# Infini-attention and GEGLU on one core: an order laid out with margins towards TensorE, score passes that share four PSUM banks, two buffers for phi of Q, and first projections that begin with high parts

## The chip, the cores and the metric

The kernel runs on one core of a Trainium2 chip. Its engines run side by side, each through its own list of instructions in program order: TensorE (PE, with a weight loader, PEld), VectorE (DVE), ScalarE (ACT), GpSimd (POOL) and SyncE (SP), which here issues the DMA transfers. They meet at semaphores. TensorE writes into PSUM, eight banks of 128 partitions by 512 float32 values; VectorE and ScalarE read them there. The metric is the device time of one execution in microseconds (us), as a median over runs.

## The reference

A layer norm, attention in four segments of 512 rows with a memory carried from segment to segment, a residual, a second layer norm, a feed-forward layer with a gate, a residual. There are 2048 rows of 512 features and 32 heads of 16 features; the feed-forward layer is 1376 wide.

```python
for s in range(N):                                   # N = 4 segments, L = 512
    qs, ks, vs = q[:, :, s], k[:, :, s], v[:, :, s]
    logits = jnp.einsum("bhqd,bhkd->bhqk", qs, ks) * scale + mask
    p = _softmax(logits, axis=-1)
    a_dot = jnp.einsum("bhqk,bhkd->bhqd", p, vs)
    pq = phi(qs)                                     # t + 1 above zero, else exp(t)
    num = jnp.einsum("bhld,bhde->bhle", pq, M)
    den = jnp.einsum("bhld,bhd->bhl", pq, z)[..., None] + 1e-6
    a_mem = num / den
    o = g * a_mem + (1.0 - g) * a_dot
    outs.append(o)
    pk = phi(ks)
    M = M + jnp.einsum("bhld,bhle->bhde", pk, vs)
    z = z + jnp.einsum("bhld->bhd", pk)
...
h = x + o @ wo
h2 = h + ((gelu(ln(h) @ w_gate) * (ln(h) @ w_up)) @ w_down)
```

All is float32. The kernel writes an operand as a high and a low part and makes a product of three matmuls (high·high, low·high, high·low; `SPLIT`).

## The kernel before

**Tiling.** Attention goes through 16 units: four groups of eight heads (`c`) by four segments (`s`), in the order of `UNITS`. A unit has two halves `Q` of four heads, 32 in all. For each unit `qkv` projects Q and K (`project`, L619: 12 matmuls of 512 columns each, for Q and for K), splits them into `hl` (L680 on ScalarE, L682 on VectorE), and spreads them by DMA over `stq` and `stk`, where a head's 16 features stand with the three parts of the split; `phi` (L627 to L631) makes the memory's feature map of Q (`pq`) and K (`pk`); `vproj` (L648) makes V for two units at a time, in `vaug`; L718 and L726 transpose phi of K and add to the memory; `mem` (L756, L772) reads it out.

**The score passes.** Each half `Q` has two. `pass_a` (L797) computes the scores once, and VectorE reduces each row to its maximum over the allowed keys (L807, 512 of them, which writes the masked scores to a scratch tile `junk` besides); the maxima are transposed (L830), copied and put into a spare row of `stq` by DMA, so that the second pass subtracts them inside its matmul. `pass_b` (L862, L869) computes the scores again, transposed; ScalarE takes the exponential out of the bank (L876), POOL zeroes what lies above the diagonal (L879), and TensorE multiplies by V in four column tiles at a time (`accum`, L900). ScalarE copies the result (L921), and it goes through DRAM to be divided by the sum.

**Banks.** A bank belongs to a pool: `PD` has three (projections, transposes, V and memory), `PA` two (scores of `pass_a`), `PB` two (scores of `pass_b`), `PPV` one (P·V). When a pool has no more use for its banks it hands them on to the feed-forward layer's pools (`PX`, `PYZ`).

**The end.** `wo_seg` (L973) multiplies by `wo`, adds the residual (L977) and stores it; `ln2` normalises, transposes (L579) and combines; `ffn` computes gate and up projections with seven block products instead of eight (L1145: 22 tiles, 42 matmuls each), with additions on VectorE (L1157) and copies on ScalarE (L1152), and the gate (L1163 to L1173); `down` (L1206, 528 matmuls) adds up in `pt` tiles (L1211).

**The start.** `ln1` normalises the rows of the first segment; its first call runs 17 transposes of no use (L497) on TensorE, then transposes the normalised rows into four banks (L568), three of `PD` and one of `PA`, and splits them into `xt` (ScalarE L588 the high part, VectorE L589 the low part).

**The order.** The program is not written in the order in which it runs. Each operation is handed to `Sched.op` with an engine, an estimated duration, a priority and its operands; `Sched.run` then plays it through and emits the instructions in the order in which they start in that play. A buffer (`Val`) takes a tile out of its pool (`Pool_`) when its first operation starts. Among the operations that could start within a short window the one of the lowest priority value goes. `DUE` shifts the priority of groups of operations (Q and K projections, DMAs, V, memory, the two passes, P·V and so on), one number for each unit or half. `LAT` is the planned time from the end of an operation on one engine to the start of its successor on another, `TAKEN` the time until its buffers are free. On the chip nothing of these times is executed: an instruction waits for its semaphores alone, in the order that came out.

## Time and profile before

| | us |
|---|---|
| median of 3 runs | 832.03 |
| lowest and highest | 831.11, 833.02 |
| profiled execution | 830.79 |
| its span, first to last instruction | 829.1 |

| engine | busy us in the span |
|---|---|
| TensorE, matmuls | 805.0 |
| TensorE, weight loads | 623.6 |
| VectorE | 612.0 |
| ScalarE | 563.5 |
| GpSimd | 484.2 |

A row of a group of instructions reads: line, engine, operation, output and inputs, shape, count, then busy time, mean ns of one, and the idle time of the engine ahead of them with what ended it. A row of the list of waits reads: who waited, for whom, us in total, number of waits, longest. A row of the timeline reads: start, length, engine, line, operation, count, and in brackets the idle time before it. A row of the windows reads: stretch, its length, then for PE, PEld, DVE, ACT and POOL the busy time and the number of instructions, the granted clock, the share of the DMA engines and GB/s. A matmul's end is modelled and reaches over the start of the next, so that busy time on PE also holds short waits; the distance from start to start is what it takes.

### The profile page before, as it was taken

Reading aid. Unit: us, or ns where it says so; the run is one execution under the profiler, and the core shown is the slowest. Engines: PE = TensorE matmul, PEld = TensorE weight load, DVE = VectorE, ACT = ScalarE, POOL = GpSimd, SP = SyncE. Lnnn points to the kernel's source line nnn. Section 1 sums busy time; section 2 is a strip of 40 time slices with the busy share of each in tenths; the row PEclk is TensorE's granted clock in tenths of the full one; section 3 lists DMA queues with packets and bytes.
Section 4 is the critical chain, followed back from the end, with each engine's and each line's share of the span. In section 5 each row is a group of like instructions: output and inputs, shape, how many; then the busy total and the mean of one; then the engine's idle time right before and its main releaser. Section 6 shows DMA issues by size and latency. Waiting matters only on the chain.

```text
span 829.1 us, 15346 instructions
## 1 busy us (share of the span) xinstructions
PE 805.0 (97%) x4709; PEld 623.6 (75%) x4709; DVE 612.0 (74%) x1831; ACT 563.5 (68%) x1127; POOL 484.2 (58%) x719
## 2 busy tenths in 40 slices
PE   5999999999999999999999999999999999999998
PEld 4877767777777677776667677777888887788886
DVE  7888678788895878888896874676568856756565
ACT  6877868689988768776776862787467464545551
POOL 7533433444445444544736895788697686778750
PEclk9999999999999999999999999999999999999999
DMA  6543534565456564556554665531111341212102
GB/s 229 148 133 94 153 108 130 151 182 155 118 156 177 159 154 119 154 152 169 165 163 144 200 200 166 164 115 48 55 55 48 95 162 51 65 39 63 51 1 102
DMA packets 71750, 103.52 MB, mean 125 GB/s; under 512 B 14324, under 2 KB 24884, under 8 KB 71668
## 3 DMA queue, kind: packets, MB, share of 16 engines
q1 hardware_dynamic: 71668, 102.54, 42.6%
q8 instruction: 37, 0.61, 0.3%
q14 instruction: 45, 0.37, 0.2%
HBM read 54.92 MB, written 21.43 MB: 92 GB/s over the span
## 4 chain that ended last, share of the span: by engine, by line
PE 77%; DVE 10%; ACT 4%; issue 3%; POOL 3%; DMA 2%; SPq 1%; ACTq 0%; POOLq 0%; DVEq 0%
PE bank L1145 19%; PE bank L1206 14%; PE bank L619 8%; PE bank L797 8%; PE bank L869 7%; PE bank L900 7%; PE bank L973 4%; PE bank L648 4%; DVE junk L807 3%; ACT pt L876 1%; PE bank L726 1%; POOL raw L1122 1%; PE bank L772 1%; PE bank L579 1%; DVE hl L682 1%
## 5 line engine op out<-in xcount | busy, mean ns | idle before, releaser
L807 DVE CUSTOM_DVE_ANT_0 junk<-bank,amask 128x256 f32<-128x256 f32 (+3 forms) x512 | 228.3, 485 | 43.4 <-PE bank L797 40.3
L879 POOL TENSOR_SCALAR_AFFINE_SELECT pt<-pt 128x128 f32<-128x128 f32 (+2 forms) x352 | 118.8, 346 | 191.6 <-ACT pt L876 183.5
L876 ACT ACTIVATE pt<-bank 128x512 f32<-128x512 f32 (+1 forms) x352 | 181.4, 560 | 42.8 <-PE bank L869 36.4
L797 PE MATMUL bank<-stk,stq 128*128 128x512 f32 (+2 forms) x384 | 128.1, 377 | 4.3 <-DVE nm L807 3.9
L869 PE MATMUL bank<-stq,stk 128*128 128x384 f32 (+2 forms) x384 | 110.8, 351 | 1.7 <-ACT pt L876 1.4
L619 PE MATMUL bank<-xt,w 128*128 128x512 f32 x384 | 108.4, 394 | 1.1 <-DVE xt L589 1.1
L1211 DVE TENSOR_TENSOR pt<-pt,bank 128x512 f32<-128x512 f32 x96 | 65.0, 685 | 41.7 <-PE bank L1206 40.1
L797 PEld LDWEIGHTS bank<-stk,stq 128*128 128x128 f32 x384 | 68.6, 188 | 28.4 <-DVE nm L807 13.8
L869 PEld LDWEIGHTS bank<-stq,stk 128*128 128x128 f32 x384 | 67.3, 188 | 19.9 <-ACT pt L876 8.3
L619 PEld LDWEIGHTS bank<-xt,w 128*128 128x128 f32 x384 | 70.4, 188 | 12.5 <-DVE xt L589 1.3
L900 PE MATMUL bank<-pt,vaug 128*32 128x512 f32 (+3 forms) x1024 | 77.0, 436 | 0.0
L900 PEld LDWEIGHTS bank<-pt,vaug 128*32 128x32 f32 x1024 | 28.9, 109 | 39.1 <-issue 30.2
L648 PE MATMUL bank<-wv,xt 128*128 128x256 f32 x384 | 54.9, 283 | 0.0
L648 PEld LDWEIGHTS bank<-wv,xt 128*128 128x128 f32 x384 | 52.2, 189 | 1.8 <-issue 0.2
L1145 PE MATMUL bank<-xt,w 128*128 128x512 f32 (+1 forms) x186 | 51.2, 391 | 0.4 <-DVE n L1171 0.4
L1115 POOL TENSOR_TENSOR w<-raw,w 128x512 fp32r<-128x512 f32 (+3 forms) x37 | 42.0, 1137 | 6.8 <-ACT w L1113 6.6
L435 POOL TENSOR_TENSOR w<-raw,w 128x512 fp32r<-128x512 f32 (+1 forms) x23 | 29.7, 1291 | 22.3 <-ACT w L430 22.1
L807 DVE DVE_READ_ACCUMULATOR2_ANT nm<- 128x1 f32 x512 | 42.0, 82 | 0.0
L1145 PEld LDWEIGHTS bank<-xt,w 128*128 128x128 f32 (+1 forms) x186 | 34.3, 186 | 8.9 <-ACT ge L1163 0.8
L1145 PE MATMUL bank<-stk,w 128*128 128x512 f32 (+1 forms) x138 | 38.8, 390 | 0.0
L1122 POOL TENSOR_TENSOR raw<-raw,raw 128x256 f32<-128x256 f32 (+1 forms) x44 | 35.2, 799 | 2.9
L1122 POOL TENSOR_TENSOR raw<-raw 128x256 f32<-128x256 f32 (+1 forms) x44 | 33.6, 765 | 1.8
(298 smaller groups left out, 1798.5 us busy)
## 6 DMA issues: line engine op xcount, KB each, us to landing
stq<-hl SPq DMA_DIRECT2D x96, 128.0 KB
stk<-hl SPq DMA_DIRECT2D x192, 64.0 KB
pv_dram<-pvs SPq DMA_DIRECT2D x32, 256.0 KB
r<-r_dram SPq DMA_DIRECT2D x28, 256.0 KB
row<-x SPq DMA_DIRECT2D x24, 256.0 KB
raw<-wg SPq DMA_DIRECT2D x20, 256.0 KB
raw<-wu SPq DMA_DIRECT2D x20, 256.0 KB
raw<-wd SPq DMA_DIRECT2D x20, 256.0 KB
```

Source lines behind the costliest of these rows:

```text
L619: nc.tensor.matmul(pm.t, w.t[:, wi, dc * P:(dc + 1) * P], XT[s][dc].t[:, xi, :], start=dc == 0 and n == 0, stop=dc == ND - 1 and n == 2)
L648: nc.tensor.matmul(pm.t[:, 256 * t:256 * t + 256], XT[s][dc].t[:, xi, t0:t0 + P], whl[wi].t[:, h, 256 * (dc % 2):256 * (dc % 2) + 256], st ...
L797: nc.tensor.matmul(sa.t[:, k * w:(k + n) * w].rearrange("x (n w) -> x n w", n=n), sq.t[:, p, i * P:(i + 1) * P], sk.t[:, p, a:a + n, 0:w], ...
L807: nc.vector.tensor_tensor_reduce(out=junk.t[:, :w], in0=sa.t[:, k * w:(k + 1) * w], in1=amask[:, D - w:], op0=OP.add, op1=OP.min, scale=-1 ...
L869: nc.tensor.matmul(sc.t[:, lo:lo + D - q0], sk.t[:, p, a, q0:q0 + P], sq.t[:, p, q0:D], start=True, stop=True)
L876: act(w, prio, lambda: nc.scalar.activation(e.t[:, :w], sc.t[:, :w], AF.Exp), [sc], [e])
L879: nc.gpsimd.affine_select(v, v, pattern=pat + [[1, P]], compare_op=OP.is_ge, fill=0.0, base=0, channel_multiplier=-1)
L900: nc.tensor.matmul(pv.t[32 * n:32 * n + 32, kb * P:D], va.t[:, kb, 17 * j:17 * j + 32], e.t[:, lo:lo + D - kb * P], start=kb == 0, stop=la ...
L1122: pool(0.14 + 2.13e-3 * h, prio, lambda: nc.gpsimd.tensor_tensor(d.t[:, d0:d0 + h], a.t[:, a0:a0 + h], c.t[:, c0:c0 + h], op=o), ins, [d])
L1145: nc.tensor.matmul(dst.t[:w], v.t[:, wi, c0 + j * w:c0 + (j + 1) * w], b[bk][j].t[:, xi, :], start=first and j == 0 and n == 0, stop=j == ...
L1206: nc.tensor.matmul(pm.t, HH[p, f, s][hi].t[:w, t * P:(t + 1) * P], v.t[:w, wi, :], start=f == fl[0] and n == 0, stop=f == fl[-1] and n == 2)
L1211: dve(D, prio, lambda a=a, pm=pm: nc.vector.tensor_tensor(a.t, a.t, pm.t, op=OP.add), [pm], [a])
```

## The change

- `DUE` has new numbers throughout.
- In `LAT`, the times from ScalarE, VectorE and GpSimd to TensorE are 0.4 us longer; in `TAKEN`, ScalarE and VectorE hold a buffer 0.1 us longer. Planned durations of the DMAs of 64 to 128 KB, of P·V and of the warm-up are others.
- `PA` and `PB` are one pool of four banks.
- `pass_a` writes the masked scores back into the score bank; `junk` keeps one buffer, for the layer norms. `pq` gets a second buffer; a scratch value of the start moves to the buffer of `e`; `pt` tiles are given out in order.
- The first layer norm runs 12 transposes of no use instead of 17, and its rows are transposed into three score banks and one of `PD`.
- Unit 0 projects Q and K together (`project_two`): for each block of features four matmuls with the high part of `xt`, then two with the low part.
- `phi` is given its output, which is taken when the projection starts.

```diff
 LAT = {
     "PE": {"PE": 0.0, "ACT": 0.27, "DVE": 0.246, "POOL": 0.24, "SP": 0.25},
-    "ACT": {"PE": 0.14, "ACT": 0.12, "DVE": 0.137, "POOL": 0.172, "SP": 0.12},
-    "DVE": {"PE": 0.108, "ACT": 0.12, "DVE": 0.17, "POOL": 0.165, "SP": 0.12},
-    "POOL": {"PE": 0.085, "ACT": 0.08, "DVE": 0.09, "POOL": 0.12, "SP": 0.12},
+    "ACT": {"PE": 0.54, "ACT": 0.12, "DVE": 0.137, "POOL": 0.172, "SP": 0.12},
+    "DVE": {"PE": 0.508, "ACT": 0.12, "DVE": 0.17, "POOL": 0.165, "SP": 0.12},
+    "POOL": {"PE": 0.485, "ACT": 0.08, "DVE": 0.09, "POOL": 0.12, "SP": 0.12},
 }
-TAKEN = {"PE": 0.22, "ACT": 0.14, "DVE": 0.12, "POOL": 0.1}
+TAKEN = {"PE": 0.22, "ACT": 0.24, "DVE": 0.22, "POOL": 0.1}
...
-    PA = Pool_(banks[3:5], then=PX)
-    PB = Pool_(banks[5:7], then=PYZ)
+    PA = PB = Pool_(banks[3:7], then=Parts(1, PX, PYZ, PX, PYZ))
...
-    PPT = Pool_(many("pt", 2, [P, D]), then=PACC)
+    PPT = Pool_(many("pt", 2, [P, D]), fifo=True, then=PACC)
     PROW1 = Pool_(many("pt1", 9, [P, D]), then=PPT)
-    PJ = Pool_(many("junk", 2, [P, D]), then=PC)
+    PJ = Pool_(many("junk", 1, [P, D]), then=PC)
     PE_ = Pool_(many("e", 1, [P, D]), then=PC)
-    PPQ = Pool_(many("pq", 1, [P, D]), then=PC)
+    PPQ = Pool_(many("pq", 2, [P, D]), then=PC)
...
-            pe(17 * 0.227, prio, lambda: [nc.tensor.transpose(
-                wm.t[0:24, 0:P], bn.t.rearrange("p t k -> p (t k)"), ident) for n in range(17)],
+            pe(12 * 0.21, prio, lambda: [nc.tensor.transpose(
+                wm.t[0:24, 0:P], bn.t.rearrange("p t k -> p (t k)"), ident) for n in range(12)],
...
-            pts = [Val(PA if dc == 3 else PD) for dc in range(ND)]
+            pts = [Val(pool_) for pool_ in ((PA, PA, PB, PD) if not behind else (PD, PD, PD, PA))]
...
+    def project_two(prio, w, s, acq):
+        pm = [Val(PD), Val(PD)]
+        for dc in range(ND):
+            def f(dc=dc):
+                for n, (i, wi, xi) in enumerate((i, wi, xi) for wis, xi in (((0, 1), 0), ((0,), 1))
+                                                for i in range(2) for wi in wis):
+                    nc.tensor.matmul(pm[i].t, w[i].t[:, wi, dc * P:(dc + 1) * P], XT[s][dc].t[:, xi, :],
+                                     start=dc == 0 and n in (0, 2), stop=dc == ND - 1 and n > 3)
+            pe(6 * mm(D), prio, f, [*w, XT[s][dc]], pm, acq=acq if dc == 0 else [])
+        return pm
...
-                junk = Val(PJ)
-
-                def g(k=k, a=a, p=p, junk=junk):
+                def g(k=k, a=a, p=p):
                     nc.vector.tensor_tensor_reduce(
-                        out=junk.t[:, :w], in0=sa.t[:, k * w:(k + 1) * w], in1=amask[:, D - w:],
+                        out=sa.t[:, k * w:(k + 1) * w], in0=sa.t[:, k * w:(k + 1) * w], in1=amask[:, D - w:],
                         op0=OP.add, op1=OP.min, scale=-1.0, scalar=BIG,
                         accum_out=nm.t[:, a, p, i:i + 1])
-                dve(w, prio, g, [sa, vamask], [junk, nm], chain=True)
+                dve(w, prio, g, [sa, vamask], [nm], chain=True)
```

## Prediction

> **What bounds the kernel now.** I read the page first, then the chain of waits in order of time, then the list of waits by engine, and last the timeline at the places that the change touches.

> ```profile
> span 829.1 us, 15346 instructions
> ...
> PE 805.0 (97%) x4709; PEld 623.6 (75%) x4709; DVE 612.0 (74%) x1831; ACT 563.5 (68%) x1127; POOL 484.2 (58%) x719
> ...
> PE   5999999999999999999999999999999999999998
> ...
> PEclk9999999999999999999999999999999999999999
> ```

> TensorE is the bound in every slice but the first, and its clock is granted in full. So the question is how much of its 805 us is work and how much is waiting that looks like work, since a matmul's recorded span contains the pipeline's tail. The unbroken stretches of the chain give the pace of each kind of matmul (columns: start, length, what):

> ```profile
> 7.61 3.58 PE bank L497 x17
> ...
> 106.33 2.29 PE bank L900 x32
> ...
> 141.69 0.71 PE bank L648 x6
> ...
> 225.60 0.87 PE bank L579 x8
> ...
> 236.19 0.86 PE bank L772 x2
> 237.99 0.93 PE bank L726 x8
> ...
> 601.84 12.26 PE bank L1145 x54
> ...
> 812.99 12.25 PE bank L1206 x54
> ```

> 12.26/54 is 0.227 us for a moving operand of 512 columns, 0.71/6 is 0.118 for 256, in proportion 0.170 for 384, and 0.87/8 is 0.109 for a transpose. The counts follow from the loops of the code. Of 512 columns: 384 (L619), 192 (L797), 128 (L869), 192 (L973), 924 (L1145) and 528 (L1206), together 2348, or 533.0 us. Of 384: 256, 43.5 us. Of 256: 640, 75.5 us. The P·V products L900: 32 groups of 2.29, 73.3 us. L726 and L772: 12 of 0.93 and 12 of 0.86, 21.5 us. Transposes 208, with the 48 short products of L756 counted as such (an upper bound), 27.9 us. The warm-up L497 3.4 us. The sum is 778 us. TensorE runs from 7.61 to 812.99 + 12.25 = 825.24, which is 817.6 us. So about 39.5 us are lost between matmuls, and that is all that an order can win: no matmul of the computation is removed. Where the named part of it lies:

> ```profile
> PEld bank L797 <- DVE nm L807: 13.8, 32, 1.7
> PEld bank L869 <- ACT pt L876: 8.3, 24, 1.0
> ...
> PEld bank L830 <- DVE pk L631: 2.4, 3, 1.6
> PEld bank L862 <- ACT pt L876: 2.3, 5, 0.9
> PEld bank L830 <- DVE mm L826: 1.6, 4, 0.5
> ...
> PEld bank L1145 <- ACT vaug L1152: 1.2, 2, 0.7
> ...
> PEld bank L1206 <- DVE ln L554: 1.0, 1, 1.0
> ```

> These are total, times and longest. The weight loader (PEld) waits for VectorE and ScalarE 71 times in these rows, 30.6 us, 0.43 us a time, nearly all in the two score passes. Its idle time is an upper bound of what TensorE loses, as a load may wait while an earlier matmul still streams. The lower bound is TensorE's own idle time: 829.1 − 805.0 = 24.1, less 7.6 before its first matmul and 3.9 after its last, leaves 12.6 us, 1.1 of it at the start (below), so 11.5.

> **The change part by part.**

> *Start (shorter warm-up, other banks for the transposed rows, the first two projections together).*

> ```profile
> 9.80 1.45 DVE L533 TENSOR_SCALAR pt<-pt,mv,ln 128x512 f32<-128x512 f32 x3
> 9.92 0.82 ACT L545 ACTIVATE pt<-pt,ln,ln 128x512 f32<-128x512 f32 x1 [0.52 <-DVE ln L539]
> ...
> 11.02 1.91 PE L568 MATMUL bank<-ident,pt 128*128 128x128 f32 x16
> ...
> 12.64 2.07 ACT L588 ACTIVATE xt<-bank 128x512 fp32r<-128x512 f32 x4 [1.91 <-PE bank L568]
> ...
> 13.27 2.48 DVE L589 TENSOR_TENSOR xt<-bank,xt 128x512 fp32r<-128x512 f32 x4 [1.42 <-ACT xt L588]
> 14.02 5.75 PE L619 MATMUL bank<-xt,w 128*128 128x512 f32 x24 [1.08 <-DVE xt L589]
> ```

> The transposes L568 start when the 17 warm-up transposes are through, at 11.02. Five fewer, at 3.58/17 = 0.21, end them about 1.05 us earlier; but the third normalised row is ready only at 9.80 + 1.45 = 11.25, and eight transposes (0.87) stand behind it, so the last ends near 12.15 rather than 12.64: 0.45 us. Then L619 waits 1.08 us for the first low part (13.27 + a quarter of 2.48, and the way), because its bank is one that the transposed rows hold. In the changed order those rows lie in three score banks and one projection bank, both projections find free banks, and four matmuls of high parts come ahead of the first with a low one (4 × 0.227 = 0.91 us of cover, against 0.69 for VectorE's one). The first matmul then needs only the first ScalarE eviction: 12.2 + 0.52 + the way, 12.85 rather than 14.02. **Term A: −1.1 us**; −1.6 if everything behind it moves up by all of the warm-up too, −0.3 if the second layer norm, which VectorE finishes at 26.5, takes most of it back.

> *The clock.* The shorter warm-up could also cost something.

> ```profile
> 7.60:10.40 2.80, 2.79 (x14) 1.90 (x15) 2.42 (x14) 2.26 (x4) 0.00 (x0) 1.00 1.05 388
> 10.40:10.80 0.40, 0.40 (x4) 0.26 (x3) 0.40 (x2) 0.33 (x1) 0.01 (x1) 1.00 1.05 405
> ```

> Fourteen transposes in the first 2.8 us, then four in 0.4 us: TensorE doubles its pace about 2.8 us after its first instruction, although the window's clock column (behind POOL's) shows 1.00. Twelve at 0.2 end at about 10.1, and the data transposes follow as the first row comes at 9.80 + 0.48, so I count nothing. If the small hole put the doubling off by another 2.8 us, half of that, 1.4 us, would be lost, which eats term A. [...]

> *Margins, new due times, four shared score banks (B).* The latencies towards TensorE in the planner rise by 0.4 us, and the release of a bank by 0.1. This costs nothing by itself: a planned pause is not executed, an instruction goes when its semaphores allow. It only makes the planner put other matmuls between a producer and its consumer. Whether it did is seen in the order of instructions, without any time of it: between the last matmul into a score bank and the next one into the same bank I add the matmuls that stand there at the paces above. For the maxima pass (352 such turnovers) the median goes from 1.54 us of work before to 2.33 after; for the exp pass from 1.37 to 1.65. The shortest turnovers that the trace of before shows are 0.3 to 0.36 us over the eviction itself:

> ```profile
> L807 DVE CUSTOM_DVE_ANT_0 junk<-bank,amask 128x512 f32<-128x512 f32 x128 | 85.9, 683 | 13.1 <-PE bank L797 12.3
> ```

> ```profile
> L876 ACT ACTIVATE pt<-bank 128x512 f32<-128x512 f32 x224 | 124.3, 597 | 23.9 <-PE bank L869 19.0 <-PE bank L862 3.5 <-POOL pt L879 0.4
> ```

> (1.04 for 512 columns on VectorE, 0.91 on ScalarE.) Turnovers with less than 0.4 us to spare over the shortest of their shape: 275 of 704 before, 122 after, 56% fewer. If the waits shrink in that proportion, the bounds are 0.56 × 30.6 = 17 us and 0.56 × 11.5 = 6.4 us. I take 10.5, nearer to the lower: in the trace of before many waits stand at turnovers with ample work, where the evicting engine was late with something else, and there only the general margin helps. **Term B: −10.5 us (−17 to −6.4).** One place is sure to be touched, the last pass with nothing else to run:

> ```profile
> 460.11 0.82 PE L869 MATMUL bank<-stq,stk 128*128 128x384 f32 x2 [0.47 <-ACT pt L876]
> ```

> Here two banks go to and fro; with four, TensorE runs further ahead.

> *Changes of tile mode (C).* The P·V and L756 products stand in 36 groups before and 40 after.

> ```profile
> 105.82 0.40 PE L869 MATMUL bank<-stq,stk 128*128 128x256 f32 x2
> 106.06 0.27 PE L830 MATMUL bank<-ident,mm 128*32 128x128 f32 x1
> 106.26 2.36 PE L900 MATMUL bank<-pt,vaug 128*32 128x512 f32 x32
> ```

> L830 takes 0.109 of the 0.20 to the next start, so about 0.09 is lost at the change. **Term C: 4 × 0.09 = +0.4 us.**

> *Maxima written into the score bank instead of `junk`; two buffers for phi of Q (D).*

> ```profile
> 25.00:125.00 100.00, 98.10 (x672) 74.36 (x671) 80.21 (x321) 78.81 (x162) 38.53 (x82) 1.00 0.47 126
> ```

> ```profile
> L1157 DVE TENSOR_TENSOR bank<-vaug,bank 128x512 f32<-128x512 f32 x22 | 15.2, 693 | 11.7 <-PE bank L1145 8.4 <-ACT vaug L1152 3.2
> ...
> L1157 DVE TENSOR_TENSOR vaug<-vaug,bank 128x512 f32<-128x512 f32 x9 | 6.2, 687 | 1.3 <-PE bank L1145 1.3
> ```

> The same addition takes 6 ns longer into a bank than into SBUF. For 512 reductions that is 3 us of VectorE, which has 20 us free in 100 there (third busy column). On TensorE's path it would be at most 352 turnovers × 6 ns = 2.1 us, and it can't be a gain beyond the freed buffer. The second phi buffer removes no wait that stands above 1 us in the list. **Term D: 0 (0 to +2.1).** DMA sizes and counts stay.

> **Sum.** −1.1 − 10.5 + 0.4 = −11.2 us. The profiled run took 830.8 us (1.7 around the span); the median of the runs shown is 832.0, so 820.8, **821 us**.

> **The rivals.**

> *All of the margin works:* B at 17 and A at 1.6 with C, −18.2, **814 us**. For it: the average wait of 0.43 us is hardly more than the 0.4 added. Against: the loader's idle time overstates.

> *The prices are paid:* clock +1.4 and D +2.1 come on top, −7.7, **824 us**.

> *The waits only move:* the order is new but another late engine sets each pause, and the change doesn't do what it says; A and C alone, −0.7, **831 us**. For it: waits at turnovers with ample work. Against: VectorE and ScalarE idle a fifth of the time in the attention stages.

> *Slower, one pass starves the other:* with one pool of four banks the maxima pass can hold all four. An exp bank then waits behind four reductions of 0.683, not two: 1.37 us each time, and ScalarE, POOL and L900 after it. Eight times among the 32 passes eat the 11.2 us; 11 times give +15.1 − 11.2, **836 us**. For it: the new order has runs of four and five matmuls of L797 together. Against: the exp pass's turnovers got longer in work, not shorter. ScalarE's present wait for the exp pass's matmuls would grow with each starving:

> ```profile
> ACT pt L876 <- PE bank L869: 36.4, 66, 2.7
> ```

> **How the numbers follow.** Forecast 0.55; all works 0.17; prices paid 0.08; waits move 0.08; starving 0.12. About 0.2% (1.7 us) can be told from no change. Faster is the first three and a fourth of "waits move", 0.82; same 0.05; slower 0.13. The forecast's own range goes from −18.2 to −0.3 − 6.4 + 0.4 + 2.1 = −4.2: 814 to 828. The range from 812 (half of the 39.5 us won) to 832 takes in the case that waits move and leaves out the starving one.

> **What would show it.** Right: the loader's waits of L797 for VectorE fall from 13.8 to some 6, those of L869 for ScalarE from 8.3 to 4; TensorE's first projection starts before 13.1; the feed-forward stage from 560 us on keeps its length. Wrong: A fails if twelve transposes are followed by data transposes at 0.2 us or the first projection still starts at 14; B fails if those waits stay above 25 us together or appear under another name (a DMA, POOL); D fails if the reduction's 683 ns grow by more than 20. The span would then be over 822 us, and with waits of ScalarE for L869 above the 36 us of before, the starving rival holds.

## The result and the profile after

| | us |
|---|---|
| before, median of 4 runs | 832.08 |
| after, median of 4 runs (852.03 to 853.61) | 852.76 |
| after, profiled execution | 852.1 |
| its span | 850.4 |

The change made the kernel slower: 1.0249 times the time before, 95% interval 1.0231 to 1.0267, or 20.7 us. The forecast was 821 us with a range of 812 to 832, and 852.8 lies outside it. The page of the changed kernel, its first lines and the chain by engine and line:

```profile
span 850.4 us, 15251 instructions
...
PE 821.1 (97%) x4704; PEld 622.4 (73%) x4704; DVE 637.5 (75%) x1831; ACT 557.4 (66%) x1127; POOL 483.2 (57%) x719
...
PE 68%; DVE 26%; issue 2%; ACT 2%; DMA 2%; SPq 0%; POOL 0%; ACTq 0%; DVEq 0%; POOLq 0%
PE bank L1160 24%; DVE bank L822 15%; PE bank L1221 14%; PE bank L884 6%; PE bank L618 5%; PE bank L915 5%; PE bank L988 4%; PE bank L814 4%; DVE nm L822 2%; PE bank L659 2%; PE bank L578 1%; PE bank L789 1%; DVE hl L701 1%; ACT pt L891 1%; PE bank L877 1%
```

The chain of the kernel before, by engine:

```profile
PE 77%; DVE 10%; ACT 4%; issue 3%; POOL 3%; DMA 2%; SPq 1%; ACTq 0%; POOLq 0%; DVEq 0%
```

TensorE runs the same matmuls less the five of the warm-up (4709 to 4704), yet is "busy" 16 us longer: the trap that the prediction named, a modelled end that covers a wait. The engine that grew is VectorE, by 25.5 us with the same 1831 instructions, and its share of the chain went from 10% to 26%. The line numbers have moved, mostly by 15: the reduction L807 is L822, the maxima pass L797 is L814, the exp pass L869 is L884.

Which matmuls wait, from the list of waits of the changed kernel (us in total, times, longest):

```profile
PEld bank L884 <- DVE nm L822: 22.8, 45, 1.1
...
PEld bank L814 <- DVE nm L822: 18.7, 44, 1.6
...
PEld bank L884 <- ACT pt L891: 5.6, 17, 0.7
```

The prediction wanted 6 in the row of the maxima pass (13.8 before). It is 18.7, and a row that did not stand in the list before is now the largest: the exp pass, which by the program has nothing to do with the maxima, waits for VectorE 45 times, because both passes take banks from one pool. The two rows together are 41.5 us, 27.7 more than the 13.8; with ScalarE's 5.6 it is 47, where the prediction called its term B wrong above 25.

To weigh TensorE's loss without the modelled ends, I took in the traces the distance from each matmul's start to the next and subtracted the paces of the prediction. Before, 39.4 us are lost between the first matmul and the last (the prediction's sum gave 39.5); after, 62.1. Between 20 and 420 us of work (attention) it is 30.0 and 54.2; from there on (mostly the feed-forward stage) 5.5 and 2.8. So the loss lies in the attention, and the feed-forward stage became a little better.

What made VectorE longer, by groups of one shape in the changed kernel:

```profile
L822 DVE CUSTOM_DVE_ANT_0 bank<-bank,amask 128x512 f32<-128x512 f32 x128 | 85.9, 712 | 20.5 <-PE bank L814 20.5
L822 DVE DVE_READ_ACCUMULATOR2_ANT nm<- 128x1 f32 x512 | 71.1, 139 | 0.0
...
L822 DVE CUSTOM_DVE_ANT_0 bank<-bank,amask 128x256 f32<-128x256 f32 x128 | 54.7, 447 | 5.3 <-PE bank L814 3.1
L822 DVE CUSTOM_DVE_ANT_0 bank<-bank,amask 128x128 f32<-128x128 f32 x128 | 39.3, 307 | 5.0 <-PE bank L814 1.7
```

and in the kernel before:

```profile
L807 DVE DVE_READ_ACCUMULATOR2_ANT nm<- 128x1 f32 x512 | 42.0, 82 | 0.0
L807 DVE CUSTOM_DVE_ANT_0 junk<-bank,amask 128x128 f32<-128x128 f32 x128 | 29.9, 286 | 4.2 <-PE bank L797 4.0
```

One reduction of 512 columns is 29 ns longer (683 to 712), the read of its accumulator 57 ns. Neither is the main price, since the two overlap with neighbours; that is seen in the starts. The four reductions of one bank with 128 columns each, on VectorE's timeline of the kernel before:

```profile
103.74 0.29 DVE L807 CUSTOM_DVE_ANT_0 junk<-bank,amask 128x128 f32<-128x128 f32 x1
103.95 0.08 DVE L807 DVE_READ_ACCUMULATOR2_ANT nm<- 128x1 f32 x1
103.95 0.28 DVE L807 CUSTOM_DVE_ANT_0 junk<-bank,amask 128x128 f32<-128x128 f32 x1
104.16 0.08 DVE L807 DVE_READ_ACCUMULATOR2_ANT nm<- 128x1 f32 x1
104.16 0.29 DVE L807 CUSTOM_DVE_ANT_0 junk<-bank,amask 128x128 f32<-128x128 f32 x1
```

and of the changed one:

```profile
216.09 0.30 DVE L822 CUSTOM_DVE_ANT_0 bank<-bank,amask 128x128 f32<-128x128 f32 x1
...
216.30 0.14 DVE L822 DVE_READ_ACCUMULATOR2_ANT nm<- 128x1 f32 x1
...
216.48 0.30 DVE L822 CUSTOM_DVE_ANT_0 bank<-bank,amask 128x128 f32<-128x128 f32 x1
...
216.69 0.14 DVE L822 DVE_READ_ACCUMULATOR2_ANT nm<- 128x1 f32 x1
...
216.87 0.30 DVE L822 CUSTOM_DVE_ANT_0 bank<-bank,amask 128x128 f32<-128x128 f32 x1
...
217.28 0.50 PE L884 MATMUL bank<-stq,stk 128*128 128x512 f32 x1 [0.58 <-DVE nm L822]
```

Before, each starts with the accumulator read of the one in front of it (103.74, 103.95, 104.16: 0.21 apart). After, they start 0.39 apart, and the gap between the read's end and the next start (216.44 to 216.48) says that the next one waits for the previous one to finish. The cause on offer: the four write the same tile, the score bank, and each waits for the writer ahead of it, where before they wrote two `junk` tiles in turn. The semaphores in the trace fit. In both kernels the later reductions of a bank carry a wait for a semaphore that VectorE's own accumulator reads raise; after, each of the 96 with 128 columns starts 0.033 to 0.035 us behind the end of the read in front of it, before most start 0.08 us ahead of that end. Over all neighbours in one bank the median distance of the starts went from 0.211 to 0.392 us for 128 columns and from 0.345 to 0.556 for 256. Banks with 128 columns hold four reductions and those with 256 two, so 96 + 64 = 160 of the 512 reductions have a neighbour to wait for: 96 × 0.18 + 64 × 0.21 = 31 us more of VectorE from start to start (its busy time, which leaves out the gaps, grew by 25.5). Right behind them, at 217.28, stands a matmul of the exp pass that has waited 0.58 us.

At the start (TensorE's timeline of the changed kernel), the first projection L630 is Q and K of unit 0 together:

```profile
7.21 2.72 PE L496 MATMUL bank<-ident,bn 128*24 128x128 f32 x12 [7.21 <-DVE bn L490]
...
9.99 2.98 PE L567 MATMUL bank<-ident,pt 128*128 128x128 f32 x16
...
13.33 5.74 PE L630 MATMUL bank<-xt,w 128*128 128x512 f32 x24 [0.36 <-ACT xt L587]
```

From the start of the warm-up it takes 6.12 us to the first projection, 6.41 before (7.61 to 14.02). In these two runs 0.3 us are won, not 1.1.

### The profile page after: what moved, and what is told of

It is laid out like the page before. It is cut to its first block, busy times and chain, and to the rows that moved or that the text cites. A ratio compares the mean times of both kernels' runs of the same rounds, so it can differ in the third digit from the quotient of the medians.

```text
span 850.4 us, 15251 instructions
## 1 busy us (share of the span) xinstructions
PE 821.1 (97%) x4704; PEld 622.4 (73%) x4704; DVE 637.5 (75%) x1831; ACT 557.4 (66%) x1127; POOL 483.2 (57%) x719
## 4 chain that ended last, share of the span: by engine, by line
PE 68%; DVE 26%; issue 2%; ACT 2%; DMA 2%; SPq 0%; POOL 0%; ACTq 0%; DVEq 0%; POOLq 0%
PE bank L1160 24%; DVE bank L822 15%; PE bank L1221 14%; PE bank L884 6%; PE bank L618 5%; PE bank L915 5%; PE bank L988 4%; PE bank L814 4%; DVE nm L822 2%; PE bank L659 2%; PE bank L578 1%; PE bank L789 1%; DVE hl L701 1%; ACT pt L891 1%; PE bank L877 1%
## 5 line engine op out<-in xcount | busy, mean ns | idle before, releaser
L822 DVE CUSTOM_DVE_ANT_0 bank<-bank,amask 128x256 f32<-128x256 f32 (+3 forms) x512 | 241.8, 513 | 44.0 <-PE bank L814 38.5
L891 ACT ACTIVATE pt<-bank 128x512 f32<-128x512 f32 (+1 forms) x352 | 172.4, 571 | 28.9 <-PE bank L884 25.2
L814 PE MATMUL bank<-stk,stq 128*128 128x512 f32 (+2 forms) x384 | 112.6, 381 | 6.1 <-DVE nm L822 5.5
L884 PE MATMUL bank<-stq,stk 128*128 128x384 f32 (+2 forms) x384 | 111.5, 370 | 7.0 <-DVE nm L822 5.2
L618 PE MATMUL bank<-xt,w 128*128 128x512 f32 x360 | 103.1, 396 | 0.0
L884 PEld LDWEIGHTS bank<-stq,stk 128*128 128x128 f32 x384 | 63.4, 188 | 38.8 <-DVE nm L822 22.8
L814 PEld LDWEIGHTS bank<-stk,stq 128*128 128x128 f32 x384 | 67.0, 189 | 32.9 <-DVE nm L822 18.7
L822 DVE DVE_READ_ACCUMULATOR2_ANT nm<- 128x1 f32 x512 | 71.1, 139 | 0.0
L915 PEld LDWEIGHTS bank<-pt,vaug 128*32 128x32 f32 x1024 | 28.7, 110 | 41.5 <-issue 37.3
L434 POOL TENSOR_TENSOR w<-raw,w 128x512 fp32r<-128x512 f32 (+1 forms) x27 | 35.2, 1308 | 35.7 <-ACT w L429 27.1
L1130 POOL TENSOR_TENSOR w<-raw,w 128x512 fp32r<-128x512 f32 (+2 forms) x34 | 40.3, 1189 | 7.7 <-ACT w L1128 7.2
L1130 POOL TENSOR_TENSOR stk<-raw,stk 128x512 fp32r<-128x512 f32 (+3 forms) x26 | 28.9, 1115 | 23.2 <-ACT stk L1128 16.1
L936 ACT ACTIVATE pvs<-bank 128x512 f32<-128x512 f32 x32 | 19.1, 596 | 30.2 <-PE bank L915 17.1
L1160 PE MATMUL bank<-stk,w 128*128 128x512 f32 x129 | 36.1, 389 | 0.0
```

Source lines behind the costliest of these rows:

```text
L618: nc.tensor.matmul(pm.t, w.t[:, wi, dc * P:(dc + 1) * P], XT[s][dc].t[:, xi, :], start=dc == 0 and n == 0, stop=dc == ND - 1 and n == 2)
L814: nc.tensor.matmul(sa.t[:, k * w:(k + n) * w].rearrange("x (n w) -> x n w", n=n), sq.t[:, p, i * P:(i + 1) * P], sk.t[:, p, a:a + n, 0:w], ...
L822: nc.vector.tensor_tensor_reduce(out=sa.t[:, k * w:(k + 1) * w], in0=sa.t[:, k * w:(k + 1) * w], in1=amask[:, D - w:], op0=OP.add, op1=OP. ...
L884: nc.tensor.matmul(sc.t[:, lo:lo + D - q0], sk.t[:, p, a, q0:q0 + P], sq.t[:, p, q0:D], start=True, stop=True)
L891: act(w, prio, lambda: nc.scalar.activation(e.t[:, :w], sc.t[:, :w], AF.Exp), [sc], [e])
L915: nc.tensor.matmul(pv.t[32 * n:32 * n + 32, kb * P:D], va.t[:, kb, 17 * j:17 * j + 32], e.t[:, lo:lo + D - kb * P], start=kb == 0, stop=la ...
```

## The experiments

The theory: writing the maxima back into the score bank makes neighbours wait, and this is nearly all of the loss. Rivals: the shared pool starves one of the two passes; the new order itself is worse; the shorter warm-up costs clock. Unless a new plan is named, the order of instructions is that of the kernel that was edited. Ratios are to the kernel before, on the same chip.

### Where the maxima are written

**e1_sbuf_out.** After, with the masked scores in two SBUF tiles by turns (`junk`, and `ge` of the feed-forward stage).

```diff
-                        out=sa.t[:, k * w:(k + 1) * w], in0=...
+                        out=next(spare)[:, :w], in0=...      # spare = cycle(junk_t + ge_t)
```

> The changed kernel in its own order, instruction by instruction, but the maxima pass writes its masked scores alternately into two tiles of SBUF instead of back into the score bank. Theory I (writing into the bank makes reductions of one bank wait for each other, 211 to 392 ns start to start for 128 columns and 345 to 554 for 256 columns, 160 of 512 reductions, some 30 us of VectorE; TensorE waits for it): VectorE's pace of before comes back, the loader's waits of L814 and L884 for VectorE fall from 18.7 + 22.8 to under 16 us, and the time to 820 to 828 us. Theory II (the new order itself, or the shared banks): the pace comes back, the time stays above 845 us.

**e2_before_inplace.** The reverse: the kernel before, its maxima written back into the bank.

```diff
-                        out=junk.t[:, :w], in0=...
+                        out=sa.t[:, k * w:(k + 1) * w], in0=...
```

> The kernel of before in its own order, but the maxima pass writes its masked scores back into the score bank. Theory I: VectorE is slowed in the same way here; slower by 15 to 30 us, 847 to 862 us. Theory II: at most the 2 us of the longer writes, 832 to 834 us.

Measured: e1 833.36 us, ratio 1.0016 (1.0000 to 1.0033): 19.4 us of the 20.7 are gone, though it stays above the expected 820 to 828, with 12.3 and 8.2 us in its two rows of waits for the maxima. e2 847.56 us, 1.0182 (1.0156 to 1.0208): this one edit costs the old order 15 us. Its list of waits:

```profile
PEld bank L797 <- DVE nm L807: 26.5, 55, 1.7
```

13.8 became 26.5 with old due times, old pools and the old warm-up. So the write-back is a cause in either order, and needs no shared pool.

**e4_inplace_single and e5_inplace_multi.** Which part of the write-back? e4 takes the SBUF tiles only for reductions with neighbours in their bank (`i < 2`, 256 of the 512), and leaves the other 256 in the bank; e5 does the opposite.

```diff
+                        out=next(spare)[:, :w] if i < 2 else sa.t[:, k * w:(k + 1) * w], in0=...   # e4
+                        out=next(spare)[:, :w] if i > 1 else sa.t[:, k * w:(k + 1) * w], in0=...   # e5
```

> The changed kernel in its own order; only the reductions that have a bank to themselves (512 and 384 columns, 256 of 512) write back into it, those that share a bank (256 and 128 columns) write into SBUF tiles. Theory I with the wait between neighbours of one bank as the price: nearly all comes back, 822 to 832 us. Theory I with the write into PSUM as the price (30 ns longer, result read 57 ns longer): half or less comes back, 838 to 848 us. Theory II: above 845 us.

> The mirror image of the last one: in the changed kernel's own order the 256 reductions that share a bank with others (256 and 128 columns) write back into it, the 256 that have one to themselves write into SBUF tiles. If the wait between neighbours of one bank is the price, nearly all of it stays: 845 to 853 us. If it is the longer write into PSUM, half of the 19 us between the changed kernel and its SBUF version goes: 838 to 844 us.

Measured: e4 **828.55 us, 0.9954 (0.9930 to 0.9977), faster than both kernels**; e5 850.65, 1.0223 (1.0200 to 1.0246), about as after. Groups of e4:

```profile
L822 DVE CUSTOM_DVE_ANT_0 bank<-bank,amask 128x512 f32<-128x512 f32 x128 | 85.9, 712 | 17.7 <-PE bank L814 17.7
...
L822 DVE DVE_READ_ACCUMULATOR2_ANT nm<- 128x1 f32 x512 | 56.1, 110 | 0.0
```

The single reductions still take 712 ns, and the mean read of 110 ns is the middle between 82 and 139: half of them still pay the price of a write into PSUM, and it costs nothing that can be seen. The wait between neighbours is the price. (In the new order, with the shared pool, it is 24.2 us, from after to e4; in the old order, with separate pools, the write-back costs 15.0. Whether the sharing or the order makes the 9 us between them is not separated.) The waits of e4 and of e5:

```profile
PEld bank L814 <- DVE nm L822: 9.8, 34, 0.5
...
PEld bank L884 <- DVE nm L822: 7.2, 18, 0.8
PEld bank L884 <- ACT pt L891: 6.1, 21, 0.7
```

```profile
PEld bank L884 <- DVE nm L822: 21.4, 46, 1.1
...
PEld bank L814 <- DVE nm L822: 17.6, 38, 1.9
```

e1 is 4.8 us slower than e4 although it writes nothing into the bank. On its timeline the reductions wait for ScalarE, which uses `junk` in the layer norms (the last brackets):

```profile
207.60 0.56 DVE L822 CUSTOM_DVE_ANT_0 junk<-bank,amask 128x384 f32<-128x384 f32 x1 [0.17 <-ACT junk L476]
...
211.97 0.42 DVE L822 CUSTOM_DVE_ANT_0 junk<-bank,amask 128x256 f32<-128x256 f32 x1 [0.49 <-ACT junk L476]
```

That these waits are the whole 4.8 us is argued, not shown.

**f4_before_one_tile.** Is it the bank, or the same tile? The kernel before, with all 512 reductions writing one SBUF tile.

```diff
-                        out=junk.t[:, :w], in0=...
+                        out=ge_0[0][:, :w], in0=...
```

> The kernel of before in its own order with all 512 reductions writing into one and the same SBUF tile instead of two by turns. If a reduction waits for the one before because both write one tile, wherever it lies, all 512 do so here, start to start 0.18 us longer (611 to about 790 ns for 512 columns), 90 us of VectorE, which is 80% busy: 60 us or more slower, 890 to 930 us. If the wait belongs to PSUM alone, 832 to 833 us.

Measured: 857.48 us, 1.0305 (1.0286 to 1.0323). The loss is there with nothing written to PSUM, though far smaller than the expected 60 us or more. Its waits, its read of the accumulator, and its starts:

```profile
PEld bank L797 <- DVE nm L807: 37.6, 83, 1.8
```

```profile
L807 DVE DVE_READ_ACCUMULATOR2_ANT nm<- 128x1 f32 x512 | 41.9, 82 | 0.0
```

```profile
109.24 0.29 DVE L807 CUSTOM_DVE_ANT_0 ge<-bank,amask 128x128 f32<-128x128 f32 x1
...
109.57 0.29 DVE L807 CUSTOM_DVE_ANT_0 ge<-bank,amask 128x128 f32<-128x128 f32 x1
...
109.91 0.29 DVE L807 CUSTOM_DVE_ANT_0 ge<-bank,amask 128x128 f32<-128x128 f32 x1
```

0.33 apart instead of 0.21, with the short read of 82 ns. So there are two things: the wait for the previous writer of the same tile (0.12 us for 128 columns), and, where that tile is in PSUM, a writer that finishes later (0.06 more).

**f1_two_places.** Can the neighbours do with one SBUF tile and the bank? e4, with the first of two reductions of 256 columns in `ge` and the second in the bank; those of 128 columns in `ge` and `junk` by turns.

```diff
+                        out=next(spare)[:, :w] if i == 0 else ge_t[0][:, :w] if i == 1 and k == 0 else sa.t[:, k * w:(k + 1) * w], in0=...
```

> The version at 828.6 us, with its use of the layer norm's scratch tile cut down: of two reductions in one bank the first writes to a free SBUF tile and the second into the bank, and only the four of 128 columns still alternate between the free tile and the scratch tile. If the reductions that waited for ScalarE's layer norm there cost what the stretch of the second layer norm lost (some 3 us more than before between 180 and 220 us of work), 825 to 827 us; if not, 828 to 829 us.

Measured: 831.30 us, 0.9991 (0.9977 to 1.0004), worse than e4 and than either expectation. The second of a pair starts 0.46 us behind the first (median; 0.345 in e4), where the first alone takes 0.425: it writes the bank that the first one has just read, and a start 0.035 behind that one's end fits a wait for it.

### The warm-up

**e3_warm17** and **f2_before_warm12.** After with 17 transposes again, and the kernel before with 12.

```diff
-                wm.t[0:24, 0:P], ...) for n in range(12)],
+                wm.t[0:24, 0:P], ...) for n in range(17)],       # e3; f2 the reverse
```

> The changed kernel in its own order with 17 instead of 12 transposes of no use at the start. If the shorter warm-up puts the doubling of TensorE's pace off (the 16 data transposes took 2.98 us after it and 1.91 before), these take 1.9 us again and the time is 0 to 1.5 us shorter, 851 to 853 us. If the warm-up doesn't matter, the five transposes are 1.0 us in the way: 853 to 854 us. No theory expects more from it.

> The kernel of before in its own order with 12 instead of 17 transposes of no use. By the prediction's term A the five take 1.05 us, of which 0.45 us can be won: 831.4 to 832.0 us. If the data transposes then run at half pace for as long as the five would have taken (2.98 us for 16 in the changed kernel), no change within 0.1%.

Measured: e3 850.62 us, 1.0217 (1.0191 to 1.0243), an interval that overlaps that of after; f2 831.69, 0.9996 (0.9983 to 1.0008). f2 is no change that could be told. e3 lies 2.1 us below after, at the edge of that; all four runs of after show a granted clock of 0.996 to 0.998, those of e3 0.999 to 1.000, and one window at half clock, as the profiled run of after has it (last section), costs up to 1.7 us. TensorE's timeline of e3 shows what the length does at the start:

```profile
8.32 3.78 PE L496 MATMUL bank<-ident,bn 128*24 128x128 f32 x17 [8.32 <-DVE bn L490]
11.90 2.06 PE L567 MATMUL bank<-ident,pt 128*128 128x128 f32 x16
14.32 5.75 PE L630 MATMUL bank<-xt,w 128*128 128x512 f32 x24 [0.36 <-ACT xt L587]
```

With 17 the data transposes take 2.06 us, with 12 they take 2.98: what the warm-up saves, they give back at half pace. From the warm-up's start to the first projection it is 6.00 us with 17 and 6.12 with 12. One run of each could mislead, for the moment of the full pace varies. In all 15 traces the transposes start 0.213 us apart (median) up to the point where the trace's record of the clock begins with the full clock, and 0.109 from there on. That point lies 3.2 to 5.4 us behind the first transpose in the five traces with 17, and 3.8 to 5.8 in the ten with 12. The ranges overlap, so no effect of the warm-up's length on that point can be told; the five more only stand in the half-paced time ahead of it.

### How much a late VectorE is worth at all

**g1_half_maxima and h2_half_maxima_new.** Half of the maxima pass's reduction is left out: each goes over the first half of its columns. g1 is the kernel before, h2 is e4.

```diff
-                        out=junk.t[:, :w], in0=sa.t[:, k * w:(k + 1) * w], ...
+                        out=junk.t[:, :w // 2], in0=sa.t[:, k * w:k * w + w // 2], ...    # g1; h2 likewise
```

> The kernel of before in its own order, its 512 reductions over the first half of their columns only (the other half of the maxima pass is left out), which takes some 100 us from VectorE. If the waits for VectorE in the old order were worth what term B takes for them (loader 13.8 + 2.4 + 1.6 us, half of it real), 820 to 824 us. If TensorE's loss is mostly something else that an order with more room between a matmul and its reduction can't win, 826 to 830 us.

> The version at 828.6 us in its own order, with its reductions over the first half of their columns only (the other half of the maxima pass is left out). In the old order this won 6.2 us. If the margins took up the waits for VectorE, at most 2 us are left to win: 826 to 829 us. If the waits stayed and only moved to the exp pass's banks, as much as in the old order or more: 818 to 823 us.

Measured: g1 825.92 us, 0.9924 (0.9906 to 0.9942), 6.2 us less than before; h2 822.43, 0.9880 (0.9852 to 0.9908), 6.1 us less than e4. g1 falls just between its two expectations; h2 is in the range of waits that stayed and only moved. Waits of g1 and of h2:

```profile
PEld bank L869 <- ACT pt L876: 8.9, 26, 1.0
...
PEld bank L797 <- DVE nm L807: 6.6, 15, 0.9
```

```profile
PEld bank L884 <- ACT pt L891: 6.2, 20, 0.9
...
PEld bank L884 <- DVE nm L822: 2.7, 6, 0.7
...
PEld bank L814 <- DVE nm L822: 1.6, 6, 0.4
```

VectorE can be given this much time in either order for the same 6 us, so the margins did not cure the waits for it (h2 would have won less than g1). What the loader's rows are worth is read by what they lost. In g1 the row of the maxima went from 13.8 to 6.6, 7.2 us less for 6.2 us of time; in h2 the two rows went from 17.0 to 4.3, 12.7 less for 6.1. Where the edit added waits, the rows rose nearly as much as the time: 12.7 for 15.0 in e2, 23.8 for 25.4 in f4, and 24.5 for 24.2 from e4 to after. So a microsecond in these rows was worth from half to about one of the kernel's.

### Margins and banks

**m02_shared, m02_split, m05_shared.** e4 with 0.2 or 0.5 us instead of 0.4 in the planned latencies towards TensorE; m02_split gives each score pass two banks again. Planned anew, with the due times of the change.

```diff
-    "ACT": {"PE": 0.54, ...}, "DVE": {"PE": 0.508, ...}, "POOL": {"PE": 0.485, ...}
+    "ACT": {"PE": 0.34, ...}, "DVE": {"PE": 0.308, ...}, "POOL": {"PE": 0.285, ...}     # m02; m05: 0.64, 0.608, 0.585
-    PA = PB = Pool_(banks[3:7], then=Parts(1, PX, PYZ, PX, PYZ))
+    PA = Pool_(banks[3:5], then=PX)                                                     # m02_split
+    PB = Pool_(banks[5:7], then=PYZ)
```

> The version at 828.6 us (reductions that share a bank write to SBUF) with margins towards TensorE of 0.2 instead of 0.4 us in the planner, all else the same; the order is planned anew. If margins bring what I predicted (about 10 us for 0.4), 832 to 836 us. If the margin is worth little, 827 to 831 us, and the loader's waits for VectorE and ScalarE stay within 3 us of that version's 23.1.

> The same with margins of 0.2 us and the score banks in two pools of two again (due times unchanged). Against the shared pool at the same margins: if sharing helps, 2 to 6 us slower (834 to 838 us); if one pass starves the other through the shared pool, faster (820 to 826 us); if neither, within 2 us.

> The version at 828.6 us with margins of 0.5 instead of 0.4 us, planned anew. If margins bring what I predicted, 825 to 828 us; if they are worth little, 828 to 832 us.

Measured: 877.93 us, 1.0555 (1.0536 to 1.0573); 863.59, 1.0380 (1.0356 to 1.0404); 846.26, 1.0169 (1.0144 to 1.0195). The smaller margin costs 49 us and the larger 18, and all three miss their expectations, so this is no measure of a margin: with these due times each of the other plans is worse by more than a margin was thought to be worth. That the due times suit 0.4 alone is the likely reason, and not shown. Nor does the pair of m02 tell what sharing is worth, beyond that in one bad plan separate banks are 14.3 us better. Margins alone and a shared pool alone in the kernel before were not tried.

## Why the prediction was wrong

**Term D, "0 (0 to +2.1)", is the step that failed.** It took the price of the write-back from one row, the addition that is 6 ns longer into a bank than into SBUF, as a price for each instruction. But the edit also made 160 pairs of neighbours write one tile. The row of L1157 could not show that, having no neighbours of that kind; what could was the row of 128-column reductions with its starts 0.21 apart beside a length of 0.29: neighbours overlapped by 0.08, and an order between them would end that. Measured: +31 us of VectorE (worked out from the starts), 24.2 us of the kernel's time from after to e4, 15 in the old order. That VectorE has 20 us free in 100 was true, and covered only the rest, for the added time comes in bursts: four reductions of a bank take 1.6 us instead of 0.84 (four times 0.39 and 0.21), while the matmuls that want that bank stand in a fixed order. The test that it named, the reduction's 683 ns growing by more than 20, did fire (712), but not for its reason: e4 shows that this growth alone costs nothing that can be seen.

**Term B, −10.5, was mis-sized, by more than its own bounds (−17 to −6.4).** e4 has the whole change but its write-back between neighbours, and gains 0.46%, 4 us, all terms together. The step that failed is "shrink in that proportion". The longer turnovers were counted in the order of instructions, but the waits did not follow them: the named rows of the two score passes are 9.8 + 7.2 + 6.1 = 23.1 us in e4, against 13.8 + 8.3 = 22.1 before. As the rival "the waits only move" has it, those for VectorE moved to the exp pass. That the loader's rows overstate, which the prediction held against its upper bound, counts for less: where they fell, they were worth half to nine tenths. By the starts, TensorE loses 30.4 us in e4's attention (30.0 before). What is won lies at its end, where the prediction expected four banks to help (380 to 420 us of work: 8.3 to 6.1), and in the feed-forward stage (5.5 to 2.6). f2, which has the order of before, loses 9.9 and 4.6 there, so single traces scatter by 1 to 2 us and part of this may be scatter.

**Term A, −1.1, was mis-sized: −0.3 in the two profiled runs.** Its working let the warm-up end earlier and the data transposes run at full pace; most of them ran at half. The clock paragraph had set aside just this case. It also read the doubling as 2.8 us after the first transpose: the single starts of before keep their 0.213 us up to 10.76, and the clock's record begins at 10.84, so it is 3.2 us. Over all traces the way from the warm-up to the first projection is 5.7 to 6.5 us for the changed start with 12 transposes (nine traces) and 6.4 to 7.5 for the old one with 17 (four), 0.8 us less on average. Little of it is left further on: from the warm-up's start to L578 (L579 before) it is 17.74 us before (7.61 to 25.35) and 18.09 after (7.21 to 25.30), and the averages over the same traces are 18.23 and 18.05.

**Term C** could not be told apart at 0.4 us.

**The starving rival** ended on the right side for another reason. Its sign was right: the exp pass did wait behind VectorE's reductions, 22.8 us in the loader's row. But its price was four reductions at 0.683 with sharing as the cause, and e4 shares the same banks in the same order without the loss, while e2 has a loss with split banks. In e2 only the maxima pass waits for VectorE's maxima; with the shared pool both passes do. Whether sharing also makes the loss larger (24.2 against 15.0) is open. The mark set for this rival, ScalarE's waits for the exp pass above 36, did not appear:

```profile
ACT pt L891 <- PE bank L884: 25.2, 49, 2.6
```

**The feed-forward stage** kept its length or better, as said.

Open: why the start-to-start loss in e4's attention before its end is 2.6 us larger than before despite the longer turnovers (it lies between 180 and 220 us of work, 1.8 before, 1.7 in f2 and 5.0 in e4), and what margins and sharing are worth apart.

## What to carry to other kernels

Before an output is moved to save a buffer, ask who wrote that tile last and whether that writer is the neighbour on the same engine: two scratch tiles by turns can be worth more than the tile that they cost. A price per instruction doesn't cover an edit that adds an order between instructions; read the distance from start to start, and where it is shorter than the length (0.21 beside 0.29 us here) there is an overlap to lose. An engine with a fifth of its time free hid here only a quarter to a half of some 30 us added, because it came in bursts ahead of matmuls in a fixed order. And more planned work between a matmul and its consumer is no proof that a wait goes: read the row of waits again, and halve the suspected work to see what that row is worth.

## What the runs showed of the hardware

**The clock halved after a stretch in which TensorE did work, but little.** Windows of the changed kernel (PE, PEld, DVE, ACT, POOL busy, then the granted clock):

```profile
227.20:230.60 3.40, 3.36 (x16) 2.21 (x15) 3.23 (x9) 3.40 (x10) 2.79 (x8) 1.00 0.55 161
230.60:234.00 3.40, 2.01 (x8) 1.06 (x7) 3.26 (x10) 3.33 (x8) 3.05 (x7) 1.00 0.70 172
234.00:237.40 3.40, 3.40 (x14) 1.14 (x16) 3.23 (x18) 2.43 (x4) 0.00 (x0) 0.50 0.73 182
237.40:241.00 3.60, 3.60 (x43) 2.21 (x36) 2.44 (x9) 1.21 (x4) 0.00 (x0) 1.00 0.22 55
```

Eight matmuls ran in the window from 230.6, and TensorE waited 1.29 us for VectorE in it; the next 3.4 us were granted half (0.50). This costs at most 1.7 us, half of 3.4, and the profiled runs of before and e4 have no such window. m02_shared, with four such stretches and 34 us at half, loses up to 17 of its 46 us so; its longest:

```profile
210.50:224.10 13.60, 7.92 (x32) 5.35 (x33) 11.71 (x48) 5.31 (x12) 0.00 (x0) 0.50 0.20 52
```

**A reduction that wrote the tile of the one ahead of it started later.** With two SBUF tiles by turns (before) the reductions of 128 columns start 0.211 us apart at a length of 0.286. All into one SBUF tile (f4) they start 0.33 apart, all into one bank (after) 0.39, in both 0.03 to 0.04 us behind the end of the accumulator read in front of them. The order between neighbours cost 0.12 us in f4 and 0.18 in after.
